# One split quarter in place of two, and a new order for all steps, in a fused RWKV attention and feed-forward kernel

## The chip, the core and the metric

The kernel runs on one core of a Trainium2 chip. The core has a matrix engine (TensorE, PE in the profile), three engines for elementwise work (VectorE or DVE, ScalarE or ACT, GpSimd or POOL) and an engine that mostly sends transfers (SyncE, SP). Each engine takes its own instructions strictly in the order in which the program lists them; engines wait for one another through semaphores. Transfers between device memory and the on-chip memory SBUF run on 16 DMA engines, which all queues share. The metric is the device time of one execution in microseconds.

## The reference

There are two parts. The first is a linear attention with a decaying state, over 4 batches, 8 heads, 768 time steps and a head width of 48. The second is a feed-forward layer (3072 tokens, 384 to 2048 to 384) with a smooth gate.

```python
for t in range(S):
    kt, vt, rt = (k[:, :, t].copy(), v[:, :, t].copy(), r[:, :, t].copy())
    cur = np.einsum('bhd,bhe->bhde', u[None] * kt, vt)
    y[:, :, t] = np.einsum('bhd,bhde->bhe', rt, state + cur)
    state = w[None, :, :, None] * state + np.einsum('bhd,bhe->bhde', kt, vt)
...
h = x @ w_in
g = np.where(pos, h, np.where(neg, 0.0, (h + beta) ** 2 / (4.0 * beta)))   # pos: h >= 1, neg: h <= -1
return (g @ w_out).astype(np.float32)
```

## The kernel before

Time is cut into 6 chunks of 128 steps, and the 4 batches into 2 pairs, which gives 12 groups, numbered 0 to 11. A group has two units (one batch each), so units run from 0 to 23. A unit is 128 tokens, a group 256. Within a chunk the recurrence becomes matrix products, and from chunk to chunk only a state per batch is carried.

For a group the steps are, by the names that the code and this text use:
- `load.K`, `load.R`, `loadV` (line 304): SP brings in K, R and V. Groups 0 and 1 come in two halves (192 KB), the others whole (384 KB).
- `Ks`, `Rs` (327): K and R times powers of the decay. `KU`, `RKU` (337, 344): the products whose row sums, `usum` (357), are the diagonal term. `V` (a cast, 212) and `V2` (367 or 369), V times the diagonal.
- `T` and `TT` (388, 212), in groups 0 to 2: TensorE turns Ks and Rs, and an engine copies them out. From group 3 on, SP does it with transposing transfers, `KRT.K` and `KRT.R` (398).
- `A` (406), `AT` (412, 416 or 421): the product of turned K and R, and its causal mask. `AT.n.0` is one VectorE instruction; where `AT.n.1` stands, ScalarE copies and POOL masks afterwards.
- `Sp`, `Tm`, `decay`, `sbf` (432, 476 and 484, 489, 212): the update of the state. `Y` and `y` (441 and 446, 468): the attention output. `X`, `xT` (501, 212 or 511): it is turned.
- `mm1.g.q` (526): the first layer of group g, quarter q of its 2048 columns, 12 matmuls for both units (written with a last figure of -1), or two halves, one for each unit, where the quarter is split. `relu`, `square`, `gate` (534 and 539 on ScalarE, 544 on VectorE) make the gated quarter, and `mm2.g.j.q` (554, 4 matmuls) adds its part of the second layer for unit j. `o` and `out` copy the sum and store it.

The weights are sent by POOL: `w_in` in two halves (290; half 0 holds quarters 0 and 1, half 1 quarters 2 and 3) and `w_out` in four (294).

The order of all this is a table of steps, written out as text in `ORDER`. The kernel walks through it and emits each step's instructions; each engine then has its instructions in that order. A step reads `name.arguments@engine:buffers~fillers`: the engine is D, P or A, the digits choose buffers, and the last figure is a number of matmuls on zeros put ahead of the step, to keep TensorE running. `warm.n` is n such matmuls by themselves.

```python
for token in ORDER.split():
    token, _, idles = token.partition("~")
    idle[0] = int(idles or 0)
    name, _, bufs = token.partition(":")
    name, _, e = name.partition("@")
    kind, *args = name.split(".")
    if kind == "warm":
        keep_warm(int(args[0]), *args[1:])
    elif kind in do:
        do[kind](e, [int(x, 36) for x in bufs], *[int(x) if x.lstrip("-").isdigit() else x for x in args])
```

The table itself was made outside the kernel by a planner, whose rules are not part of the file.

Of the kernel before, what the change touches and what calls it, by code (L numbers as in the profile page):

```python
# [40 lines left out]
usum.1.0@A:1 A.1:0~8 V2.0.0@P:0 Ks.2.0@P:2 AT.2.0:1 loadV.2.0:0 V2.1.0@A:1 Y.0:1 T.3:2 sbf.0@A Tm.2@D usum.0.1@D Y.2:0
TT.3@D:3 y.2:0 AT.1.1:2 Rs.2.0@P:2 A.3:1~14 X.2:0 V2.0.1@A y.0:1 AT.3.0:3 warm.2.h.2 X.0:1 T.5:2~8 AT.1.0 xT.2@A:0
T.4:0 TT.5@D:0 Y.1:0 w_in.1 load.K.3.0:0 xT.0@A:1 sbf.1@A usum.1.1@D A.5:1 mm1.0.0.0:2 KU.2.0@P:0 y.1:2 TT.4@D:1
load.R.3.0:0 V.1.1@A X.1:1 Y.3:0 AT.5.0:0 A.4:0 V2.1.1@P xT.1@A mm1.0.0.1 V.2.0@A:2 Sp.5:1 y.3:0 RKU.2.0@P:0
relu.0.0:0 X.3:0 Tm.5@D:0 mm1.0.1.0:1 AT.4.0:1 xT.3@A decay.5 square.0.0:0 usum.2.0@D:0 Sp.4:1 mm1.0.1.1 w_out.0 Y.4:0
relu.0.1:1 mm1.1.1.-1:0 gate.0.0:0 square.0.1:1 Tm.4@D:1 mm1.0.2.-1:2 relu.1.1:0 Y.5:1 square.1.1:0 V2.2.0@P:0 w_out.1
y.4:1 gate.0.1:1 w_out.2 X.4:0 w_out.3 mm1.0.3.-1:1 xT.4@A:2 gate.1.1:2 relu.0.2:1 Sp.3:0 y.5:2 mm1.1.0.-1:0
square.0.2:1 Tm.3@D KU.3.0@P:1 decay.4 gate.0.2:3 relu.0.3:0 relu.1.0:1 mm2.0.0.0:1 mm2.0.1.0:0 Ks.3.0@P:0 RKU.3.0@D:1
square.1.0:0 KRT.K.3:0 mm1.1.3.-1:2 mm2.0.1.1 Rs.3.0@P:0 mm2.0.0.1 square.0.3:1 gate.1.0:4 mm2.0.1.2 gate.0.3:5
relu.1.3:1 loadV.3.0:1 mm2.0.0.2 mm1.1.2.-1:0 square.1.3:0 usum.3.0@D:1 mm2.0.0.3 relu.1.2:0 KRT.R.3:0 mm2.0.1.3  # L50
o.0.0@D:0 square.1.2:1 mm2.1.0.0:1 o.0.1@D gate.1.3:6 load.K.4.0:1 X.5:0 mm2.1.0.1 load.R.4.0:1 xT.5@A V.3.0@A:3
mm1.2.3.-1:1 gate.1.2:7 sbf.3@A V2.3.0@P:1 Sp.7:0 A.7:2 loadV.4.0:0 relu.2.3:1 Tm.7@D:0 A.6:0 mm2.1.0.2 AT.6.0:2
sbf.2@A square.2.3:0 Ks.4.0@P:2 sbf.4@A Sp.6:0 mm2.1.0.3 load.K.5.0:2 Tm.6@D:1 mm1.2.0.-1:0 o.1.0@A:1 AT.7.0:3 decay.6
Y.6:0 Y.7:1 relu.2.0:0 KRT.K.4:1 y.6:0 mm1.2.1.-1:2 KU.4.0@P:0 y.7 V.4.0@A:4 gate.2.3:8 xT.6:1 RKU.4.0@P:0
square.2.0:1 mm2.1.1.0:0 Sp.8:1 mm2.1.1.1 load.R.5.0:2 Tm.8@D:1 relu.2.1:1 load.K.6.0:0 mm1.2.2.-1:1 gate.2.0:9
Ks.5.0@P:1 mm2.1.1.2 square.2.1:0 mm2.2.0.0:1 mm2.1.1.3 decay.7 Rs.4.0@P:1 mm1.3.0.-1:0 gate.2.1:0 relu.2.2:0
square.2.2:1 KRT.K.5:0 mm2.2.0.1 o.1.1@D sbf.5@A relu.3.0:1 mm1.3.1.-1:2 gate.2.2:1 out.1 KU.5.0@P:1 square.3.0:0
Rs.5.0@P:2 mm2.2.0.2 relu.3.1:0 gate.3.0:3 mm1.3.2.-1:1 KRT.R.4:1 square.3.1:1 loadV.5.0:1 load.R.6.0:0 usum.4.0@D:0
mm2.2.0.3 mm2.2.1.0:0 KU.6.0@P:0 relu.3.2:1 gate.3.1:5 mm1.3.3.-1:0 square.3.2:0 loadV.6.0:0 gate.3.2:4 mm2.2.1.1
V2.4.0@P:0 sbf.6@A o.2.0@A:1 A.9:2 sbf.7@A relu.3.3:0 A.8:1 AT.9.0:1 mm2.2.1.2 KRT.R.5:0 square.3.3:1 mm2.3.0.0:1  # L60
AT.8.0:0 out.0 decay.8 mm2.2.1.3 load.K.7.0:1 mm2.3.0.1 o.2.1@A gate.3.3:2 V.6.0@A:0 V.5.0@A:2 Y.8:0 Ks.6.0@P:0
mm2.3.0.2 y.8:1 Y.9:0 mm2.3.0.3 y.9 RKU.5.0@P:1 A.11:2 xT.8:0 o.3.0@A:0 A.10:1 usum.5.0@D:1 AT.11.0:2 mm2.3.1.0:0
Sp.10:1 KRT.K.6:1 mm2.3.1.1 Rs.6.0@P:0 RKU.6.0@P:0 Tm.10@D:0 mm2.3.1.2 load.R.7.0:1 Sp.9:1 mm2.3.1.3 Tm.9@D:1
V2.5.0@P:1 mm1.4.0.-1:0 AT.10.0:3 o.3.1@A sbf.8@A decay.9 decay.10 KRT.R.6:1 usum.6.0@D:0 relu.4.0:1 Sp.11:1 Y.10:0
mm1.4.1.-1:2 square.4.0:0 Tm.11@D:1 y.10:0 V2.6.0@P:0 Ks.7.0@P:2 Y.11:1 mm1.4.2.-1:1 loadV.7.0:0 out.2 relu.4.1:0
gate.4.0:7 y.11 A.12:0 xT.10:2 square.4.1:1 AT.12.0:0 mm2.4.0.0:0 Sp.12:1 relu.4.2:1 KU.7.0@P:1 square.4.2:0
gate.4.1:6 load.K.8.0:2 mm1.4.3.-1:0 V.7.0@A:1 KRT.K.7:0 gate.4.2:9 load.R.8.0:2 A.13:2 Rs.7.0@P:1 mm2.4.0.1 out.3
Tm.12@D:0 mm1.5.0.-1:1 AT.13.0:1 RKU.7.0@P:1 relu.4.3:0 square.4.3:1 relu.5.0:1 gate.4.3:0 loadV.8.0:1 square.5.0:0
sbf.9@A decay.12 mm2.4.0.2 Y.12:1 mm1.5.2.-1:2 usum.7.0@D:1 mm2.4.0.3 Ks.8.0@P:1 y.12:1 mm1.5.1.-1:0 gate.5.0:1
o.4.0@A:1 Y.13:1 KRT.R.7:0 relu.5.2:0 V2.7.0@P:1 KRT.K.8:1 Sp.13:0 square.5.2:1 mm1.5.3.-1:1 y.13 Tm.13@D:0 decay.11  # L70
relu.5.1:1 xT.12:1 gate.5.2:8 mm2.4.1.0:1 KU.8.0@P:0 Sp.14:0 square.5.1:0 mm2.4.1.1 load.K.9.0:0 Tm.14@D:1 mm2.4.1.2
relu.5.3:0 sbf.10@A gate.5.1:3 mm2.5.0.0:0 Rs.8.0@P:2 A.15:2 square.5.3:1 A.14:0 AT.15.0:3 mm2.4.1.3 mm2.5.0.1
V.8.0@A:3 KRT.R.8:1 decay.13 RKU.8.0@P:0 AT.14.0:2 mm1.6.0.-1:2 o.4.1@A load.R.9.0:0 gate.5.3:5 Y.14:1 mm2.5.0.2
Ks.9.0@P:0 y.14:0 relu.6.0:1 mm1.6.1.-1:0 square.6.0:0 usum.8.0@D:0 gate.6.0:4 loadV.9.0:0 load.K.10.0:1 mm2.5.0.3
mm2.5.1.0:1 sbf.11@A sbf.12@A A.17:1 relu.6.1:0 o.5.0@D:0 KU.9.0@P:1 A.16:2 mm2.5.1.1 AT.17.0:0 V2.8.0@P:0 decay.14
Rs.9.0@P:0 square.6.1:1 sbf.13@A Y.15:0 mm2.5.1.2 mm1.6.2.-1:1 y.15 V.9.0@A:4 AT.16.0:1 xT.14:0 KRT.K.9:0 Sp.15:0
RKU.9.0@P:1 gate.6.1:2 mm2.5.1.3 load.R.10.0:1 mm1.6.3.-1:2 relu.6.2:1 square.6.2:0 relu.6.3:0 o.5.1@D Tm.15@D:0
mm2.6.0.0:1 gate.6.2:7 out.5 Y.16:0 mm1.7.1.-1:0 decay.15 square.6.3:1 y.16:1 KRT.R.9:0 Ks.10.0@P:2 Sp.17:0 Tm.17@D:1
gate.6.3:6 load.K.11.0:2 mm2.6.0.1 relu.7.1:1 mm1.7.0.-1:1 KU.10.0@P:0 square.7.1:0 sbf.15@A mm2.6.0.2 Sp.16:0
relu.7.0:0 KRT.K.10:1 loadV.10.0:1 gate.7.1:9 mm1.7.2.-1:2 Rs.10.0@P:1 Tm.16@D:0 mm2.6.0.3 square.7.0:1 o.6.0@A:0  # L80
# [557 lines left out]
```

## Time and profile before

| what | value |
|---|---|
| median of 3 runs | 174.3 us (174.28 to 174.5) |
| the profiled execution | 174.08 us |
| its span, first to last instruction | 172.4 us |
| granted TensorE clock | 1.000 |
| TensorE busy | 163.6 us, 95% |
| VectorE, ScalarE, POOL busy | 78%, 79%, 69% |
| bytes moved by DMA | 28.78 MB |

All times in the rows are microseconds from the span's start, unless a row says ns. A row of a timeline gives start, length, engine, line, operation and what is written from what; in brackets stands how long the engine sat idle before, and what ended that. A row of a group gives the count, the time busy, the mean of one in ns, and the idle time before. The busy share of TensorE counts the matmuls on zeros as well.

### The profile page before, as it was taken

The page shows a single profiled execution, that of the slowest core. Times are in us where ns is not written, and L with a number is a line of the kernel's source. Part 1 is how long each engine was busy: PE and PEld are TensorE (multiplying, and loading weights), DVE is VectorE, ACT ScalarE, POOL GpSimd, SP SyncE. Part 2 cuts the span into 40 slices and gives each one's busy share as a digit, 9 for nine tenths or more (in the row PEclk, how much of TensorE's full clock was granted, in tenths as well). Part 3 has the DMA queues.
Part 4 walks back from the last instruction along what each step waited for, and adds up shares of the span by engine and source line. Part 5 has one row for each costly group of instructions (what it writes and reads, how often), then busy time and mean ns, then how long its engine had stood idle before and what let it go on. Part 6 is the DMA issues. An engine that isn't in the chain of part 4 may idle for free.

```text
span 172.4 us, 4127 instructions
## 1 busy us (share of the span) xinstructions
PE 163.6 (95%) x1668; PEld 123.6 (72%) x1668; DVE 133.6 (78%) x167; ACT 135.4 (79%) x194; POOL 118.2 (69%) x96
## 2 busy tenths in 40 slices
...
DMA packets 106967, 28.78 MB, mean 167 GB/s; under 512 B 100930, under 2 KB 106180, under 8 KB 106948
## 3 DMA queue, kind: packets, MB, share of 16 engines
...
q10 hardware_dynamic: 148, 0.10, 0.2%
q14 instruction: 6, 0.05, 0.1%
...
## 4 chain that ended last, share of the span: by engine, by line
PE 73%; DMA 7%; DVE 6%; POOL 5%; SPq 4%; ACT 2%; issue 1%; DVEq 0%; POOLq 0%
PE op L554 32%; PE hp L526 32%; DMA w_in_sb<-in_moe_w_in_dram 5%; SPq L304 4%; PE A L406 3%; DVE RKU L344 2%; DMA R<-in_r_dram 2%; DVE AT L421 2%; PE Y L446 2%; PE Y L441 2%; DVE gt L544 2%; PE Sp L432 1%; POOL AT L416 1%; POOL Rs L327 1%; POOL Ks L327 1%
## 5 line engine op out<-in xcount | busy, mean ns | idle before, releaser
L526 PE MATMUL hp<-xT,w_in_sb 128*128 128x256 bf16 (+1 forms) x600 | 70.8, 268 | 1.2 <-DMA w_in_sb<-in_moe_w_in_dram 0.4
L554 PE MATMUL op<-w_out_sb,gt 128*128 128x384 bf16 x384 | 71.8, 326 | 0.1
L544 DVE SCALAR_TENSOR_TENSOR gt<-sq,hp 128x1024 bf16<-128x1024 f32 x48 | 57.9, 1216 | 14.5 <-ACT sq L539 14.4
L526 PEld LDWEIGHTS <-w_in_sb 128*128 128x128 bf16 x600 | 55.6, 98 | 11.3 <-issue 1.2
L534 ACT ACTIVATE pt<-hp 128x1024 f32<-128x1024 f32 x48 | 48.7, 1019 | 12.0 <-PE hp L526 11.8
L539 ACT ACTIVATE sq<-pt 128x1024 f32<-128x1024 f32 x48 | 50.4, 1057 | 2.8 <-DVE gt L544 1.6
L554 PEld LDWEIGHTS <-gt 128*128 128x128 bf16 x384 | 35.6, 98 | 20.0 <-issue 0.6
L421 DVE TENSOR_TENSOR AT<-A,umask 128x1024 bf16<-128x1024 f32 x22 | 26.5, 1218 | 1.9 <-PE A L406 1.7
L337 POOL TENSOR_TENSOR KU<-K,u_bc 128x768 f32<-128x768 f32 (+1 forms) x13 | 21.7, 1667 | 1.8 <-DVE u_bc L212 1.8
L369 POOL TENSOR_TENSOR V<-V,diag 128x768 f32<-128x768 bf16 (+1 forms) x12 | 16.5, 1375 | 8.8 <-ACT V L212 7.1
L344 POOL TENSOR_TENSOR RKU<-R,KU 128x768 f32<-128x768 f32 (+1 forms) x13 | 20.4, 1575 | 0.4 <-DMA R<-in_r_dram 0.2
L489 POOL TENSOR_TENSOR state<-Tm,wCm 128x384 f32<-128x384 f32 x16 | 16.1, 1006 | 5.3 <-DVE Tm L476 5.1
L327 POOL TENSOR_TENSOR Ks<-Wdn,K 128x768 bf16<-128x768 f32 x10 | 18.3, 1831 | 0.9 <-DMA K<-in_k_dram 0.9
L327 POOL TENSOR_TENSOR Rs<-Wup,R 128x768 bf16<-128x768 f32 x10 | 18.3, 1826 | 0.0
L468 DVE TENSOR_TENSOR yy<-Y,V 128x384 bf16<-128x384 f32 x18 | 9.9, 553 | 5.0 <-PE Y L446 3.5
L212 ACT COPY oo<-op 128x384 f32<-128x384 f32 x13 | 6.2, 477 | 7.9 <-PE op L554 7.9
L446 PE MATMUL Y<-V,AT 128*128 128x48 bf16 x192 | 11.2, 184 | 1.2 <-POOL AT L416 0.9
L212 ACT CAST V<-VF 128x768 bf16<-128x768 f32 (+1 forms) x14 | 10.2, 736 | 2.6 <-DMA VF<-in_v_dram 2.6
L446 PEld LDWEIGHTS <-AT 128*128 128x128 bf16 x192 | 9.5, 96 | 2.7 <-POOL AT L416 1.2
L476 DVE TENSOR_TENSOR Tm<-Sp,state 128x384 f32<-128x384 f32 x16 | 8.9, 554 | 3.1 <-PE Sp L432 1.8
L357 DVE TENSOR_REDUCE diag<-RKU 128x16 f32<-128x768 f32 (+1 forms) x13 | 11.1, 851 | 0.0
L212 ACT CAST state_bf<-state 128x384 bf16<-128x384 f32 x20 | 10.0, 503 | 0.0
...
## 6 DMA issues: line engine op xcount, KB each, us to landing
out_dram<-oo SPq DMA_DIRECT2D x11, 384.0 KB, 3.1
K<-in_k_dram SPq DMA_DIRECT2D x10, 384.0 KB, 4.6
R<-in_r_dram SPq DMA_DIRECT2D x10, 384.0 KB, 4.5
VF<-in_v_dram SPq DMA_DIRECT2D x10, 384.0 KB, 5.3
...
w_out_sb<-in_moe_w_out_dram POOLq DMA_DIRECT2D x4, 384.0 KB, 7.4
K<-in_k_dram SPq DMA_DIRECT2D x4, 192.0 KB, 3.6
R<-in_r_dram SPq DMA_DIRECT2D x4, 192.0 KB, 3.9
```

Source lines behind the costliest of these rows:

```text
L212: nc.scalar.copy(out, in_) if e == "A" else engines[e].tensor_copy(out, in_)
L327: engines[e].tensor_mul(of_unit(dst, j0, j1)[:, :, :, :D], rep(tab, j1 - j0), of_unit(tiles[what, g], j0, j1))
L337: engines[e].tensor_mul(of_unit(tiles["KU", g], j0, j1), of_unit(tiles["K", g], j0, j1), rep(u_bc, j1 - j0))
L344: engines[e].tensor_mul(of_unit(tiles["RKU", g], j0, j1), of_unit(tiles["R", g], j0, j1), of_unit(tiles["KU", g], j0, j1))
L369: engines[e].tensor_mul(tiles["V2", g][:, hs, :], tiles["V", g][:, hs, :], tiles["diag", g][:, hs].unsqueeze(2).to_broadcast([P, hs.stop - ...
L421: nc.vector.tensor_mul(t.rearrange("p i n t -> p (i n) t"), tiles.pop(("A", n)).rearrange("p i n t -> p (i n) t"), umask.unsqueeze(1).to_b ...
L446: nc.tensor.matmul(t[:, 2 * p + i, :], tiles["AT", n][:, i, p, :], tiles["V", g][:, j * H + 2 * p + i, :], start=(c == 0), stop=True, skip ...
L526: nc.tensor.matmul(hp[:, f, cols], w_in_sb[:, i, n0 : n0 + P], tiles["xT", g][:, units, i, :], start=(i == 0), stop=(i == nK - 1), skip_gr ...
L534: nc.scalar.activation(tiles["pt", g, q], tiles["hp", g, q], AF.Relu, bias=0.5, scale=0.5)
L539: nc.scalar.activation(tiles["sq", g, q], tiles.pop(("pt", g, q)), AF.Square, bias=0.0)
L544: nc.vector.scalar_tensor_tensor(out=gt, in0=tiles.pop(("sq", g, q)), scalar=1.0, in1=tiles.pop(("hp", g, q)), op0=ALU.min, op1=ALU.max)
L554: nc.tensor.matmul(tiles["op", g, j], tiles["gt", g, q][:, f, j * P : (j + 1) * P], w_out_sb[:, n, :], start=(n == 0), stop=(n == nF - 1),)
```

## The change

`SPLIT` goes from 2 to 1; no line of the kernel reads it, and it records what the table was made with. The table is new from its second line on. In group 0 only quarter 0 of the first layer is still in halves, and quarter 1 is one piece. Some steps change engine: KU.0.0, RKU.0.0 and RKU.1.1 go from POOL to VectorE, RKU.3.0 from VectorE to POOL, TT of units 2, 3 and 4 from VectorE to ScalarE, usum.1.0 from ScalarE to VectorE, V2.0.1 from ScalarE to POOL, and ten of the copies of outputs between ScalarE and VectorE. The number of matmuls on zeros goes from 62 to 75. The other steps are the same ones in another order.

```diff
-SPLIT = 2
+SPLIT = 1
...
-lw loadV.0.0:0 bcw:1 load.K.1.1 KU.0.1@D loadV.0.1 wcol:0 Wdn_p:0 Ks.0.0@D:0 Wup_p load.R.1.1 Rs.0.0@D:0 wCm
+loadV.0.0:0 KU.0.0@D:0 loadV.0.1 RKU.0.0@D:0 bcw:1 wcol:0 Wdn_p:0 KU.0.1@D load.R.1.1 Wup_p Ks.0.0@D:0 KU.1.0@P:1
...
```

On POOL, from its last product of the first group's second half, up to the second half of w_in (V with a number is a V2; AFFINE_SELECT is the mask of AT; L290 sends w_in):

```order
 L344 TENSOR_TENSOR RKU<-R,KU 128x384
+L369 TENSOR_TENSOR V_254<-V,diag 128x384
+L416 AFFINE_SELECT AT<-AT 128x1024
 L290 DMA w_in_sb<-in_moe_w_in_dram 128x3x1024
-L416 AFFINE_SELECT AT<-AT 128x1024
-L369 TENSOR_TENSOR V_327<-V,diag 128x384
 L327 TENSOR_TENSOR Ks<-Wdn,K 128x16x48
 L327 TENSOR_TENSOR Rs<-Wup,R 128x16x48
 L416 AFFINE_SELECT AT<-AT 128x1024
+L369 TENSOR_TENSOR V_254<-V,diag 128x384
+L369 TENSOR_TENSOR V_343<-V,diag 128x384
 L290 DMA w_in_sb<-in_moe_w_in_dram 128x3x1024
```

The first send of w_in now comes after the V2 and the mask of unit 0, and the second after the V2 of the other half of group 0 and of the second half of group 1.

On VectorE, in groups 0 and 1 (tab holds the powers of the decay; diag is usum; state from Sp is Tm of the first chunk):

```order
 L357 TENSOR_REDUCE diag<-RKU 128x8
-L327 TENSOR_TENSOR Ks<-tab,K 128x8x48 x2
+L327 TENSOR_TENSOR Ks<-tab,K 128x8x48
+L327 TENSOR_TENSOR Rs<-tab,R 128x8x48
+L484 TENSOR_TENSOR state<-Sp,wCm 128x384
+L344 TENSOR_TENSOR RKU<-R,KU 128x384
+L357 TENSOR_REDUCE diag<-RKU 128x8
+L484 TENSOR_TENSOR state<-Sp,wCm 128x384
 L212 COPY TT<-T 128x1024
```

RKU.1.1 now stands here, behind the first state and ahead of the copy TT of unit 1. Further on, in the gates of group 0 and 1:

```order
+L468 TENSOR_TENSOR y<-Y,V_638 128x384
 L544 SCALAR_TENSOR_TENSOR gt<-sq,hp 128x1024
-L344 TENSOR_TENSOR RKU<-R,KU 128x768
+L468 TENSOR_TENSOR y<-Y,V_638 128x384
 L544 SCALAR_TENSOR_TENSOR gt<-sq,hp 128x1024 x2
```

The whole-group product RKU.3.0 is gone from between the gates.

On SP, where group 3 is turned (KT and RT) and groups 3 and 4 are loaded:

```order
 L304 DMA R<-in_r_dram 128x16x48
 L398 DMA_TRANSPOSE KT<-Ks 128x8x128
+L304 DMA K<-in_k_dram 128x16x48
 L304 DMA VF<-in_v_dram 128x16x48
 L398 DMA_TRANSPOSE RT<-Rs 128x8x128
+L304 DMA R<-in_r_dram 128x16x48
```

The load of K for group 4 now goes between the transposes of group 3, ahead of V for group 3.

More of the change, by code (lines that the diff above doesn't have):

```diff
@@ L41 @@
[L41 to L80, printed above, removed]
@@ L96 @@
-mm2.10.0.0:1 relu.11.0:0 mm2.10.1.1 square.11.0:0 square.11.1:1 mm2.10.0.1 gate.11.0:4 relu.11.2:0 mm2.10.1.2
-square.11.2:0 mm2.10.0.2 mm2.10.1.3 out.9 mm2.10.0.3 mm1.11.3.-1:1 o.10.0@D:0 o.10.1@D gate.11.1:2 out.10 mm2.11.0.0:1
-relu.11.3:1 mm2.11.1.0:0 gate.11.2:7 square.11.3:1 mm2.11.0.1 mm2.11.1.1 gate.11.3:6 mm2.11.0.2 mm2.11.1.2 mm2.11.0.3
-o.11.0@D:0 out.11.0 mm2.11.1.3 o.11.1@A:1 out.11.1
+warm.18 load.K.0.0:0 load.R.0.0:0 load.K.0.1 load.R.0.1 load.K.1.0:1 load.R.1.0:1 load.K.1.1 bcu:0 lw u_bc@D
```

81 lines of the change are left out of this document (62 added, 19 removed).

## The prediction

> **What bounds the kernel now.** I read the page first, for the span and the share of each engine, then the chain of waits in order of time, and then each engine's timeline where the chain leaves TensorE. From the page:
>
> ```profile
> span 172.4 us, 4127 instructions
> PE 163.6 (95%) x1668; PEld 123.6 (72%) x1668; DVE 133.6 (78%) x167; ACT 135.4 (79%) x194; POOL 118.2 (69%) x96
> ```
>
> TensorE (PE) is the bound by share, but the filler matmuls count in it, so I go by stretches. From the chain of waits (start, length, what):
>
> ```profile
> 8.30 3.82 DMA R<-in_r_dram
> ...
> 20.55 8.09 DMA w_in_sb<-in_moe_w_in_dram
> ...
> 28.69 1.48 PE hp L526 x12
> ...
> 34.41 3.97 DVE RKU L344
> ...
> 39.56 1.47 PE hp L526 x12
> ...
> 45.35 0.17 PE Sp L432 x4
> 45.52 0.55 PE A L406 x16
> ...
> 47.65 1.31 PE hp L526 x12
> ...
> 49.70 1.31 PE hp L526 x12
> 51.01 0.65 PE op L554 x4
> ...
> 163.50 5.21 PE op L554 x32
> 168.74 0.48 ACT o_sb L567
> ```
>
> These rows cut the span into three stretches and give each step's price on TensorE: a first-layer quarter (mm1, 12 matmuls) 1.31 us, a second-layer step (mm2, 4 matmuls) 0.65, Sp 0.17, A 0.275 (two in 0.55), and one Y 0.37 (two stand between 48.96 and 49.70).
> - Up to 28.69 TensorE waits for its first work. The last wait there is for the second half of w_in, sent at 20.55; it lets mm1.0.2 start at 28.69.
> - From 28.69 to 47.65 (mm1.2.0) lie 6 quarters, 12 mm2 steps, one Y, three Sp, two A and two X (taken as 0.17, like Sp): 7.86 + 7.80 + 0.37 + 0.51 + 0.55 + 0.34 = 17.4 of 18.96 us. So 1.5 us are stalls, and the chain shows where: RKU of group 3, 3.97 us on VectorE, holds the gate that releases the matmul at 39.56.
> - From 47.65 to the last matmul's end at 168.71 lie 39 quarters, 84 mm2 steps, 18 Y, 12 Sp and 16 A: 51.1 + 54.6 + 6.7 + 2.0 + 4.4 = 118.8 of 121.1 us, so 2.3 us are stalls. Then 3.7 us of tail.
>
> The change leaves this work as it is from mm1.2.0 on. What can differ is when mm1.2.0 starts, the later stalls, and the tail.
>
> **The change, part by part.** *The split quarter.* mm1.0.1 was two halves and becomes one piece. The timeline of PE for halves:
>
> ```profile
> 21.39 0.84 PE L526 MATMUL hp<-xT,w_in_sb 128*128 128x128 bf16 x12
> 22.07 0.33 PE L501 MATMUL X<-ident,y 128*128 128x128 bf16 x3
> ```
>
> A half takes 0.68 us from start to start, two take 1.36 against 1.31: 0.05 us. It lies ahead of a wait (below), so I count nothing. The 13 further fillers (75 for 62, at 0.06 to 0.11 us each) stand ahead of waits too: nothing.
>
> *When the weights are sent.* This is the main term. POOL sends w_in, in its order, and before it ran so:
>
> ```profile
> 13.20 0.93 POOL L290 DMA_DIRECT2D w_in_sb<-in_moe_w_in_dram  x1
> ...
> 15.19 0.84 POOL L369 TENSOR_TENSOR V<-V,diag 128x384 f32<-128x384 bf16 x1
> ...
> 17.75 1.82 POOL L327 TENSOR_TENSOR Rs<-Wup,R 128x768 bf16<-128x768 f32 x1
> 19.52 1.09 POOL L416 TENSOR_SCALAR_AFFINE_SELECT AT<-AT 128x1024 bf16<-128x1024 bf16 x1
> 20.55 0.80 POOL L290 DMA_DIRECT2D w_in_sb<-in_moe_w_in_dram  x1
> ...
> 28.92 2.29 POOL L294 DMA_DIRECT2D w_out_sb<-in_moe_w_out_dram  x3
> ```
>
> Now w_in.0 stands behind V2.0.0 and the mask of AT.0, and w_in.1 behind V2.0.1 and V2.1.1. POOL loses three half-size products to VectorE (KU.0.0, RKU.0.0, RKU.1.1) and gains V2.0.1 (0.84 us, as the row at 15.19), which ScalarE did. ScalarE's rows:
>
> ```profile
> 11.71 1.01 ACT L412 CAST AT<-A 128x1024 bf16<-128x1024 f32 x1
> ...
> 22.18 0.51 ACT L212 CAST V<-VF 128x384 bf16<-128x384 f32 x1 [0.82 <-DMA VF<-in_v_dram]
> ```
>
> AT.0.1 at 11.71 follows the cast of the second half of V0, whose load keeps its place in the queue, so I leave it at 11.8. Its end at 12.8, the mask's 1.1 (row at 19.52), and w_in.0 goes at 13.9 to 14.1, 0.7 to 0.9 late. Then Ks.2 (15.0) and Rs.2, each 1.82 as the row at 17.75 (to 18.6), the mask of AT.1 (19.6), V2.0.1 (20.4). V2.1.1 needs the cast V.1.1, at 22.18 before and waiting for its load. That load meets the weights. Issues on SP and issues to landing:
>
> ```profile
> 9.30 0.94 SPq L304 DMA_DIRECT2D VF<-in_v_dram  x1
> ...
> 11.06 1.73 SPq L304 DMA_DIRECT2D R<-in_r_dram  x1
> 12.83 3.55 SPq L304 DMA_DIRECT2D VF<-in_v_dram  x2
> ```
> ```profile
> VF<-in_v_dram SPq DMA_DIRECT2D x1, 192.0 KB, 3.6
> ```
> ```profile
> R<-in_r_dram SPq DMA_DIRECT2D x1, 384.0 KB, 6.3
> ```
> ```profile
> VF<-in_v_dram SPq DMA_DIRECT2D x1, 192.0 KB, 9.3
> ```
>
> V1.0 lands at 12.9 and R2 at 17.4, two loads of 384 KB later (K2 lies between): 2.2 us each. V1.1, half of that, would land at 18.5; it landed at 22.1, when w_in.0 had gone through (13.20 and the 8.1 us of w_in in the chain is 21.3). So loads of SP hardly move while weights do. With w_in.0 0.7 to 0.9 later V1.1 just misses or just makes it. I take that most of it is caught again and it lands at 21.5 to 22. Then V.1.1 ends at 22.1, V2.1.1 at 22.9, and w_in.1 goes 2.3 us late, at 22.9; with the 8.1 us of the first chain row it lands at 31.0. TensorE is ready by then: w_in.0 lands at 22.1, three quarters follow (3.9), and the steps for Y and X between them, with their casts, bring it to the end of Y.4 at about 29; this has 2 us of room and does not carry the sum. So mm1.0.2 starts at 31.0, 2.3 us late. Bounds: w_in.1 at 21.4 (V1.1 in time, POOL alone the limit), 0.9 late; and 23.5, 3 late.
>
> *From there to mm1.2.0.* Y.5 is now done ahead of mm1.0.2, and one Sp (0.17) too: 16.9 us remain. RKU.3.0 goes back to POOL, where a product of that size takes 1.83 us (row at 33.95, below), so the 3.97 us on VectorE are gone. From the page, ScalarE's two steps for a quarter (count, busy, mean ns):
>
> ```profile
> L534 ACT ACTIVATE pt<-hp 128x1024 f32<-128x1024 f32 x48 | 48.7, 1019 | 12.0 <-PE hp L526 11.8
> L539 ACT ACTIVATE sq<-pt 128x1024 f32<-128x1024 f32 x48 | 50.4, 1057 | 2.8 <-DVE gt L544 1.6
> ```
>
> That is 2.08 us a quarter. Five quarters go through ScalarE between 31.0 and the gate of mm1.1.3, which TensorE wants last, at about 47: 10.4 us of 16, with room for the small casts and the gate; I find no stall there. What is late next is group 3 on SP, where load K4 now stands between the two transposes, ahead of V3:
>
> ```profile
> 35.81 1.33 SPq L398 DMA_TRANSPOSE KT<-Ks  x1
> 37.25 0.52 SPq L304 DMA_DIRECT2D VF<-in_v_dram  x1
> 37.86 3.47 SPq L398 DMA_TRANSPOSE RT<-Rs  x1
> ```
> ```profile
> KT<-Ks SPq DMA_TRANSPOSE x1, 5.1
> ```
> ```profile
> VF<-in_v_dram SPq DMA_DIRECT2D x1, 384.0 KB, 5.4
> ```
> ```profile
> RT<-Rs SPq DMA_TRANSPOSE x1, 5.6
> ```
>
> They land in turn: KT at 40.9, V3 at 42.6, RT at 43.5; so a load of 384 KB takes about 1.8 us of the stream, a transpose 0.9. w_out's last piece was sent by 31.2 (row at 28.92); now KU.2, RKU.2, a decay, V2.2 and four sends follow w_in.1, so it is sent by about 33. The stream, busy with w_in.1 until 31.0, sets its end rather than the sending; I take 1 us later, so KT lands at 41.9, K4 at 43.7, V3 at 45.5, RT at 46.4. TensorE, without stalls, would ask for V3 (Sp.6) at 45.7; cast (0.83 us) and RT give it at 46.5. That is 0.8 us lost. mm1.2.0 starts at 31.0 + 16.9 + 0.8 = 48.7, 1.1 us late. From both sides: if the loads run as fast as they did before it is nothing, if K4 waits for w_out's end longer, 2 us.
>
> *From mm1.2.0 on.* POOL has two products of 1.8 us less left (Ks.4 and KU.4 are done earlier), so what feeds the attention steps is further ahead. I take 0.6 of the 2.3 us of stalls as gone; the ends are all of them (2.3) and 2 us more. Copies of the output that change engine are ten and balance. At the end the two units swap names and stand in the same order: nothing.
>
> **Sum:** 1.1 - 0.6 = 0.5 us. The profiled execution took 174.08 us around its span of 172.4; the median shown, 174.3, is 0.2 above it. So 174.6 for such an execution, and 174.8 as a median. The forecast's own range is 174.2 to 175.6.
>
> **The rivals.** *V1.1 slips ahead of the weights* (faster). It needs about 1.1 us more of the stream than R2, and gets 0.7 to 0.9, with R2's 17.4 already somewhat held up. If it lands by 20, w_in.1 goes at 21.5, mm1.0.2 starts at 29.6, w_out keeps its old times, and V3 and RT land at 44.6 and 45.7; mm1.2.0 then starts at 47.8, 0.15 late, and with 0.6 of stalls gone the time is 173.8. The later stalls vanishing whole would bring either case a further 1.7 us.
>
> *RKU.1.1 caught behind POOL* (slower). The product has two operands in SBUF, as the 3.97 us one had, and POOL ran two products beside that one:
>
> ```profile
> 33.95 1.83 POOL L327 TENSOR_TENSOR Ks<-Wdn,K 128x768 bf16<-128x768 f32 x1
> 35.73 1.83 POOL L327 TENSOR_TENSOR Rs<-Wup,R 128x768 bf16<-128x768 f32 x1
> ```
>
> It began at 34.41 and ended at 38.38, 0.8 us after POOL's second had ended at 37.56: it stood still until POOL paused. RKU.1.1 comes up at 12.2 (its load lands at 12.1, the first row of the chain). POOL pauses at 12.5, before AT.0's mask; a start there costs nothing. From 12.85 on POOL's queue is closed up to the end of Rs.2 at 18.6; a VectorE that is 0.4 us later than I reckon stands until then, with TT.1 and AT.2 behind it: 5.6 us, of which the 2.3 us of waiting for w_in.1 hide some: 178. [...]
>
> *ScalarE becomes the bound in groups 2 and 3* (slower). Between mm1.2.0 and mm1.3.3 TensorE has 6 quarters, 12 mm2 steps, 3 Y, 2 Sp and 2 A: 17.7 us. ScalarE has six relu and six square there, 12.5 us, and eight smaller steps, where the old order had six and five, and three smaller ones. If it comes into this stretch over 2 us behind, each gate waits for its square: about 2 us, 176.5. Against it speaks ScalarE's share, 79% on the page, and that two of the eight steps are casts whose loads come early.
>
> *It comes to nothing:* the times move within the ramp and the same end is reached, 174.0 to 174.6.
>
> **How the numbers follow.** Forecast 0.40, V1.1 in time 0.24, ScalarE 0.18, nothing 0.10, RKU.1.1 caught 0.08. The three stalls of unknown size give the range: 173.0 (V1.1 in time and half of the later stalls gone besides) to 177.3 (ScalarE with 0.8 more), which leaves out the caught RKU and a little below. No change is within 0.2% (0.35 us), about what a measurement of this kernel can tell. Faster: 0.24 and 0.06 of the forecast with all later stalls gone, 0.30. Same: 0.10 and 0.08 of the forecast's lower edge, 0.18. Slower: 0.26 + 0.18 + 0.08 = 0.52.
>
> **What would show it.** Right: POOL's second w_in issue near 22.9, V.1.1's cast waiting for its load, TensorE waiting for w_in shortly before 31, no VectorE product of several us, and a wait for V3 or RT near 46. Wrong: the second issue by 21.6 with V1.1 landed by 20; RKU.1.1 on VectorE longer than 1.5 us; ScalarE named as what the gates wait for between 49 and 66; or stalls after mm1.2.0 that sum to over 3 us.

## The result, and the profile after

The changed kernel took 177.01 us (three runs, 176.16 to 177.57) where the kernel before took 174.3. The ratio is 1.0137, with a 95% interval from 1.0104 to 1.017: slower, by 2.7 us where 0.5 was forecast. The profiled execution after took 177.01 us around a span of 175.3, so the span grew by 2.9 us. In every median and ratio here and below, executions that took over 1.5% longer than the fastest of the same kernel are left out; three of them, in two of the runs below, took 212 to 417 us.

From the page, the span, TensorE's share, and the granted clock by fortieths of the span (4.4 us each):

```profile
span 175.3 us, 4111 instructions
PE 165.0 (94%) x1669; PEld 125.5 (72%) x1669; DVE 131.2 (75%) x168; ACT 134.9 (77%) x172; POOL 117.8 (67%) x95
PEclk9999969999999999999999999999999999999998
```

The sixth digit is new (the row before was all nines): from 21.9 to 26.3 us TensorE got 0.69 of its clock. The same stretch by 2 us (length, busy time of PE, PEld, DVE, ACT, POOL with counts, clock, DMA):

```profile
22.00:24.00 2.00, 0.72 (x14) 0.64 (x14) 1.94 (x3) 1.68 (x4) 1.12 (x2) 0.90 1.12 222
24.00:26.00 2.00, 2.00 (x13) 1.36 (x10) 1.75 (x3) 0.83 (x1) 1.98 (x2) 0.50 1.22 228
26.00:28.00 2.00, 2.00 (x28) 1.85 (x26) 0.24 (x1) 1.28 (x2) 1.92 (x2) 0.75 1.18 201
```

POOL, where it sends the two halves of w_in (its timeline):

```profile
13.77 0.93 POOL L290 DMA_DIRECT2D w_in_sb<-in_moe_w_in_dram  x1
...
22.88 0.83 POOL L369 TENSOR_TENSOR V<-V,diag 128x384 f32<-128x384 bf16 x1 [2.19 <-ACT V L212]
23.65 0.80 POOL L290 DMA_DIRECT2D w_in_sb<-in_moe_w_in_dram  x1
```

The second half goes at 23.65; it went at 20.55. Ahead of it POOL stood 2.19 us for V2.1.1, that is for the cast of V1.1, which stood on ScalarE for its load. The load itself was not later than before, when the cast began at 22.18; new is what stands behind it.

```profile
22.29 0.51 ACT L212 CAST V<-VF 128x384 bf16<-128x384 f32 x1 [1.95 <-DMA VF<-in_v_dram]
22.71 0.85 ACT L212 COPY xT<-X 128x384 bf16<-128x384 bf16 x2
```

The transfer of the second half takes 8.1 us from issue to landing, so the weights are there at 31.75:

```profile
w_in_sb<-in_moe_w_in_dram POOLq DMA_DIRECT2D x1, 768.0 KB, 8.1
```

TensorE's timeline, from that wait to mm1.0.2 and then at mm1.2.0:

```profile
23.23 0.33 PE L432 MATMUL Sp<-V,Ks 128*128 128x96 bf16 x4 [1.23 <-ACT xT L212]
23.61 0.48 PE L446 MATMUL Y<-V,AT 128*128 128x48 bf16 x8
23.91 3.63 PE L526 MATMUL hp<-xT,w_in_sb 128*128 128x256 bf16 x24
...
29.63 0.20 PE L441 MATMUL Y<-state_bf,TT 128*128 128x96 bf16 x1 [0.62 <-ACT xT L212]
...
31.68 0.77 PE L204 MATMUL hp<-zeros 128*128 128x128 bf16 x11
32.30 1.91 PE L526 MATMUL hp<-xT,w_in_sb 128*128 128x256 bf16 x16
...
47.72 0.33 PE L432 MATMUL Sp<-V,Ks 128*128 128x96 bf16 x4 [0.40 <-ACT V L212]
...
50.02 1.47 PE L526 MATMUL hp<-xT,w_in_sb 128*128 128x256 bf16 x12
```

The row at 32.30 is mm1.0.2: it waits for nothing, so in this execution TensorE itself came last, 0.55 us after the weights. The chain of waits agrees (start, length, what): it leads from the load of V1.1 through ScalarE and TensorE to the matmuls on zeros ahead of mm1.0.2, and not through w_in.

```profile
13.02 9.25 DMA VF<-in_v_dram
22.29 0.51 ACT V L212
22.80 0.77 ACT xT L212 x2
...
26.69 1.03 ACT pt L534
27.74 1.06 ACT sq L539
...
29.20 0.39 ACT xT L212
...
31.84 0.62 PE hp L204 x11
```

mm1.2.0 is the last row, at 50.02. (The timeline shows it at 47.48 before; the chain of waits, by which the prediction counted, adds 0.16 or 0.17.) The increase splits like this:

| stretch | before | forecast change | after | change |
|---|---|---|---|---|
| to mm1.0.2 | 28.69 | +2.3 | 32.30 | +3.6 |
| mm1.0.2 to mm1.2.0 | 18.8 | -1.2 | 17.7 | -1.1 |
| mm1.2.0 to the span's end | 124.9 | -0.6 | 125.3 | +0.4 |

In the last stretch the only waits of TensorE that the timeline shows are for the turned R of groups 5 and 7:

```profile
72.86 0.62 PE L406 MATMUL A<-RT,KT 48*128 48x128 bf16 x16 [0.62 <-DMA RT<-Rs]
92.88 0.40 PE L406 MATMUL A<-RT,KT 48*128 48x128 bf16 x8 [0.27 <-DMA RT<-Rs]
```

### The profile page after: what moved, and what is told of

It is laid out like the page before. It is cut to its first block, busy times and chain, and to the rows that moved or that the text cites. A ratio compares the mean times of both kernels' runs of the same rounds, so it can differ in the third digit from the quotient of the medians.

```text
span 175.3 us, 4111 instructions
## 1 busy us (share of the span) xinstructions
PE 165.0 (94%) x1669; PEld 125.5 (72%) x1669; DVE 131.2 (75%) x168; ACT 134.9 (77%) x172; POOL 117.8 (67%) x95
## 4 chain that ended last, share of the span: by engine, by line
PE 53%; POOL 14%; DMA 14%; SPq 7%; ACT 6%; issue 3%; DVE 0%; POOLq 0%
PE hp L526 24%; PE op L554 23%; DMA VF<-in_v_dram 9%; SPq L304 7%; POOL Rs L327 3%; POOL Ks L327 3%; DMA RT<-Rs 3%; POOL KU L337 3%; DMA K<-in_k_dram 2%; POOL V L369 2%; POOL state L489 2%; PE A L406 2%; ACT sq L539 2%; PE Y L446 2%; PE Y L441 1%
## 5 line engine op out<-in xcount | busy, mean ns | idle before, releaser
L526 PE MATMUL hp<-xT,w_in_sb 128*128 128x256 bf16 (+1 forms) x588 | 71.9, 274 | 0.0
L554 PE MATMUL op<-w_out_sb,gt 128*128 128x384 bf16 x384 | 71.0, 326 | 0.0
L526 PEld LDWEIGHTS <-w_in_sb 128*128 128x128 bf16 x588 | 56.2, 99 | 10.1 <-DMA xT<-yy 0.3
L534 ACT ACTIVATE pt<-hp 128x1024 f32<-128x1024 f32 x48 | 49.0, 1020 | 17.5 <-PE hp L526 17.3
L421 DVE TENSOR_TENSOR AT<-A,umask 128x1024 bf16<-128x1024 f32 x22 | 26.3, 1217 | 1.9 <-PE A L406 1.8
L369 POOL TENSOR_TENSOR V<-V,diag 128x768 f32<-128x768 bf16 (+1 forms) x13 | 17.3, 1328 | 11.3 <-ACT V L212 8.2
L337 POOL TENSOR_TENSOR KU<-K,u_bc 128x768 f32<-128x768 f32 (+1 forms) x12 | 20.2, 1686 | 4.6 <-DMA K<-in_k_dram 4.6
L212 ACT COPY oo<-op 128x384 f32<-128x384 f32 x12 | 5.6, 476 | 6.3 <-PE op L554 6.3
```

The costliest lines, as they stand in the source:

```text
L212: nc.scalar.copy(out, in_) if e == "A" else engines[e].tensor_copy(out, in_)
L337: engines[e].tensor_mul(of_unit(tiles["KU", g], j0, j1), of_unit(tiles["K", g], j0, j1), rep(u_bc, j1 - j0))
L369: engines[e].tensor_mul(tiles["V2", g][:, hs, :], tiles["V", g][:, hs, :], tiles["diag", g][:, hs].unsqueeze(2).to_broadcast([P, hs.stop - ...
L421: nc.vector.tensor_mul(t.rearrange("p i n t -> p (i n) t"), tiles.pop(("A", n)).rearrange("p i n t -> p (i n) t"), umask.unsqueeze(1).to_b ...
L526: nc.tensor.matmul(hp[:, f, cols], w_in_sb[:, i, n0 : n0 + P], tiles["xT", g][:, units, i, :], start=(i == 0), stop=(i == nK - 1), skip_gr ...
L534: nc.scalar.activation(tiles["pt", g, q], tiles["hp", g, q], AF.Relu, bias=0.5, scale=0.5)
```

## The experiments

In the diffs each line is one token of the table of steps, cut to the place; dots stand for tokens left out. The table shows for every run where three marks of TensorE lie in its profile (start of mm1.0.2, start of mm1.2.0, end of the span), and the time against the kernel before on the same chip. The medians of before were 174.7 to 174.9 on those chips. Executions of one changed kernel spread by a microsecond or two. The marks are those of one profiled execution each: they show where its time went, and carry that spread too. The steps behind mm1.2.0 are the same in seven of the runs with the new order (after and six others), and there the rest alone goes from 125.3 to 127.0.

| run | mm1.0.2 | mm1.2.0 | end | rest | median | ratio and interval |
|---|---|---|---|---|---|---|
| before | 28.69 | 47.48 | 172.4 | 124.9 | 174.3 | 1 |
| after | 32.30 | 50.02 | 175.3 | 125.3 | 177.01 | 1.0137 (1.0104 to 1.017) |
| before, w_in.1 late | 32.32 | 51.72 | 176.7 | 125.0 | 177.53 | 1.0165 (1.0111 to 1.0218) |
| before, RKU.3.0 on POOL | 28.98 | 47.34 | 172.4 | 125.1 | 174.42 | 0.9979 (0.9959 to 1.0) |
| before, quarter in one piece | 29.14 | 47.81 | 173.0 | 125.2 | 174.87 | 1.0011 (0.9991 to 1.003) |
| after, w_in.1 sooner | 31.17 | 48.80 | 175.6 | 126.8 | 177.27 | 1.011 (1.0037 to 1.0183) |
| after, V1.1 hidden | 33.06 | 50.81 | 176.7 | 125.9 | 178.09 | 1.0184 (1.0143 to 1.0225) |
| after, both | 31.15 | 48.99 | 174.3 | 125.3 | 177.78 | 1.0202 (1.0163 to 1.0241) |
| after, 26 fillers | 32.23 | 49.78 | 176.8 | 127.0 | 179.34 | 1.025 (1.0202 to 1.0299) |
| after, K4 later | 32.31 | 49.87 | 176.8 | 126.9 | 178.3 | 1.0189 (1.0142 to 1.0236) |
| after, send between the V2, fewer fillers | 30.82 | 48.89 | 175.0 | 126.1 | 176.86 | 1.0107 (1.0027 to 1.0187) |
| that, and V1.1 hidden | 29.48 | 48.36 | 174.8 | 126.4 | 176.64 | 1.0101 (1.0068 to 1.0135) |
| that, and two late moves | 30.35 | 49.01 | 174.8 | 125.8 | 176.52 | 1.0113 (1.007 to 1.0157) |
| after, two late moves alone | 31.55 | 49.84 | 175.3 | 125.5 | 177.31 | 1.0195 (1.0118 to 1.0272) |

### The late send by itself

The theory to be tested first was that the late second send of w_in is the cost; the rival, that V1.1's held load is, through ScalarE and the clock. The kernel before got the late send and nothing else:

```diff
 Y.1:0
-w_in.1
 load.K.3.0:0
...
 V2.1.1@P
...
+w_in.1
```

> The kernel before with only the second send of w_in put behind KU.2 and V2.1.1 on POOL, at 23.9 us in place of 20.55. Theory A: the weights land at 32, mm1.0.2 starts 3.3 us late, of which the stall behind RKU.3.0 (its end at 38.4 does not move) takes back 1: 176.5. Theory B: the send by itself is a third of the loss at most: 175.0 to 175.5.

The send went at 23.97. TensorE's timeline:

```profile
27.48 1.47 PE L526 MATMUL hp<-xT,w_in_sb 128*128 128x256 bf16 x12
32.32 2.08 PE L526 MATMUL hp<-xT,w_in_sb 128*128 128x256 bf16 x12 [3.37 <-DMA w_in_sb<-in_moe_w_in_dram]
```

mm1.0.2 comes 3.6 us late, after a plain wait of 3.37 us for the weights, and the end is 4.3 us later (the first quarters behind the wait ran at a low clock, 0.76 from 32 to 34 us and 0.50 from 34 to 36, the first in 2.08 us against 1.47). The ratio, 1.0165, is that of the changed kernel within the uncertainty: one late send is enough for the whole increase, which speaks for theory A (176.5) and against theory B (175.5 at most).

### Curing one limit of the changed kernel, or both

First w_in.1 alone, ahead of both V2 products (sent at 20.39):

```diff
+w_in.1
 V2.0.1@P
...
 V2.1.1@P
...
 Sp.3:1
-w_in.1
```

> The changed kernel with one step moved: POOL sends the second half of w_in ahead of V2.0.1 and V2.1.1, at about 19.9 us in place of 23.65. Theory A (the late send is what costs): the weights land by 28.5, mm1.0.2 starts 2 us sooner, time 175.0. Theory B (the load of V1.1, held by the first half of w_in, stops ScalarE for 2 us and with it the start of the first layer, and TensorE's clock drops while it waits): TensorE itself reaches mm1.0.2 only at about 32, so nothing moves, 176.5 to 177.2.

Then V1.1 alone: the first quarter goes ahead of Sp.3, and ScalarE copies xT of units 2 and 1 before it casts V1.1 (w_in.1 then goes at 24.88):

```diff
-V.1.1@A
 A.5:0
 xT.2@A:1
-V2.1.1@P
...
 xT.1@A
+mm1.0.1.-1:1
+V.1.1@A
+V2.1.1@P
 Sp.3:1
...
-mm1.0.1.-1:1
```

> The changed kernel with the wait for V1.1 put behind the first quarter: ScalarE casts V.1.1 after xT of units 2 and 1, and TensorE runs mm1.0.1 before Sp.3 and Y.3. Nothing else moves. Theory A (late send): the second half of w_in still lands at 31.7, so 176.5 to 177. Theory B: mm1.0.1 starts at about 22.3 in place of 23.9 with the clock up, and TensorE then waits for w_in at mm1.0.2 until 31.8: 0.5 us gained, 176.5. By both the gain alone is small; a wait for w_in at mm1.0.2 must appear by B and not by A.

And both moves:

> Both of the two moves together. Theory A: as the sooner send alone, 175.0. Theory B: only together do they help, mm1.0.2 at about 29 in place of 32.3, 3 us gained, of which V3 and the transposed R of group 3 take back 1: 175.0. The two theories part on the sooner send alone, not here; if this too stays at 177, neither holds and the loss lies in group 3 and behind it.

With the weights sooner there was no wait for w_in, and yet mm1.0.2 started at 31.17 only, as theory B said and not theory A. This move is no clean cure, though: V2.0.1 now stood behind the send, and TensorE waited 1.10 us at 22.71 for y of unit 1, in place of the wait for V1.1. With V1.1 hidden TensorE was ready at 31.52 and stood 1.54 us for the weights, the wait that theory B asked for:

```profile
33.06 1.16 PE L526 MATMUL hp<-xT,w_in_sb 128*128 128x256 bf16 x9 [1.54 <-DMA w_in_sb<-in_moe_w_in_dram]
```

The 33.06 itself is not the price of the move: in that execution R of group 2 landed late (Rs.2 began at 18.27, in the changed kernel's profile at 17.03), and what follows on POOL and TensorE was as much later. So two limits lie within about a microsecond of each other, the weights and TensorE itself, and curing one uncovers the other. With both moves mm1.0.2 still starts at 31.15, where 29 was expected, since the wait for y of unit 1 is there as in the run with the send alone. The time stayed near 177.8 where both theories gave 175.0, so this run decides nothing between them:

```profile
22.47 0.34 PE L501 MATMUL X<-ident,y 128*128 128x128 bf16 x3 [1.11 <-DVE y L468]
...
23.69 1.47 PE L526 MATMUL hp<-xT,w_in_sb 128*128 128x256 bf16 x12 [0.55 <-DVE AT L421]
```

### The clock

In the changed kernel's profile 24 matmuls (the first quarter and half of the second) took 3.63 us, at half clock up to 27 us (0.50). The two other executions of the changed kernel kept a mean clock of 1.000 and took 176.16 and 177.57 us, so the increase does not hang on the clock. If the wait of 1.23 us ahead of the matmuls lowers it, matmuls on zeros should prevent it:

```diff
-Sp.3:1
+Sp.3:1~26
```

> The changed kernel with 26 more matmuls on zeros ahead of the state product Sp.3, where TensorE stood idle for 1.23 us before its clock fell to half. Theory: the wait for V1.1 costs through the clock; the fillers (26 at about 0.055 us, 1.4 us) lie in the idle time and keep the clock up. Then the 24 matmuls of the first quarter take about 2.15 us instead of 3.63, TensorE reaches mm1.0.2 at about 30.8 instead of 32.30, and only now waits for the second half of w_in, about 0.9 us, to 31.75: mm1.0.2 at 31.8, mm1.2.0 at 49.5, time 0.5 us less than the changed kernel's. First rival: the idle time is not what lowers the clock; the 24 matmuls take 3.6 us again, mm1.0.2 stays at 32.3 or goes to 32.5. Second rival: the weights come earlier too and the whole 1.5 us is gained, mm1.0.2 at 30.8.

```profile
23.29 1.61 PE L204 MATMUL Sp<-zeros 128*128 128x128 bf16 x26 [1.01 <-ACT xT L212]
24.73 0.33 PE L432 MATMUL Sp<-V,Ks 128*128 128x96 bf16 x4
...
25.11 2.14 PE L526 MATMUL hp<-xT,w_in_sb 128*128 128x256 bf16 x24
```

The 24 matmuls took 2.14 us, but the experiment missed its aim: the row shows that the fillers wait for the copy xT too (they write the buffer of Sp.3, which has the same figure as that of X of unit 2), and behind it they cost 1.44 us of their own. The next runs settle the question in another way. The one below has the changed order up to 39.5 us, with the same wait, longer still, and the clock stayed up:

```profile
24.05 0.33 PE L432 MATMUL Sp<-V,Ks 128*128 128x96 bf16 x4 [1.57 <-ACT xT L212]
24.64 2.14 PE L526 MATMUL hp<-xT,w_in_sb 128*128 128x256 bf16 x24
...
32.31 1.92 PE L526 MATMUL hp<-xT,w_in_sb 128*128 128x256 bf16 x16 [0.39 <-DMA w_in_sb<-in_moe_w_in_dram]
```

There mm1.0.2 waits for w_in and starts at 32.31, as late as before (the send was at 24.47). In the run with the two late moves alone, further down, it also waits for w_in, and starts at 31.55. So the low clock is no steady part of the change; with it or without it the late weights let mm1.0.2 start at 31.55 to 32.31.

### K of group 4 back behind V of group 3

```diff
-load.K.4.0:0
 square.0.3:1
...
 loadV.3.0:1
...
 KRT.R.3:0
...
+load.K.4.0:0
 Ks.4.0@P:1
```

> The changed kernel with one load moved on SP: K of group 4 goes behind V and the second transpose of group 3, not between them. Theory (a term of the prediction): K4 ahead of V3 holds V3 and RT of group 3 back by 0.8 us and TensorE waits for them ahead of mm1.2.0. Then V3 lands at about 46.0 instead of 46.8, RT at 47.0 instead of 47.8, and from mm1.0.2 to mm1.2.0 go 17.0 us instead of 17.7; time 0.8 us less than the changed kernel's. Rival: K4 then lands so late that POOL's Ks.4 (which waited 2.27 us for it already) and with it the later products on POOL slip by 2 to 3 us; the 0.8 us come back as waits for A and T after mm1.2.0, and the time stays at 177.

The wait for V3 (0.40 us in the changed kernel) is gone, but mm1.0.2 to mm1.2.0 shortens only from 17.7 to 17.6 us. Behind it the rival's waits came: 0.97 us at 54.37 behind y on VectorE and 0.86 at 74.21 for the turned R, and the rest grew to 126.9. POOL now has K of group 4 at 48.6 and starts Ks.4 3.8 us later than in the changed kernel (48.7 for 44.88).

### Two single steps done to the kernel before

RKU of group 3 on POOL, behind Rs of group 3:

```diff
 Ks.3.0@P:0
-RKU.3.0@D:1
...
 Rs.3.0@P:0
 mm2.0.0.1
+RKU.3.0@P:1
```

> The kernel before with one step of the change: the product RKU of group 3 on POOL, behind Rs of group 3, instead of on VectorE between two gates. Theory: its 3.97 us on VectorE hold a gate back and cost TensorE most of the 1.5 us of stalls between mm1.0.2 and mm1.2.0. On POOL it takes 1.84 us in idle time. Then mm1.0.2 stays at 28.7, mm1.2.0 goes from 47.5 to 46.4 (46.0 to 46.8), and the time from 174.3 to 173.2. Rival: the stall is followed by the wait for V3 and the turned R of group 3, which do not come sooner; mm1.2.0 stays within 0.3 of 47.5 and the time at 174.3.

The quarter in one piece:

```diff
-mm1.0.1.0:1
+mm1.0.1.-1:1
...
-mm1.0.1.1
```

> The kernel before with the one edit that the change's name tells of: quarter 1 of group 0's first layer in one piece instead of two halves, at the place of the first half. Theory: two halves cost 0.05 us more than one piece, both parts of xT are there by then, and it lies ahead of the wait for the weights: 174.3, mm1.0.2 at 28.7. Rival: the piece waits for xT of the second unit, or holds its PSUM buffer longer, and the first relu comes later: ScalarE and the gates of group 0 slip by up to 0.7 us, 175.0.

RKU.3.0 on POOL takes mm1.0.2 to mm1.2.0 from 18.8 to 18.4 us, not the 1.1 us less that was expected. There was little more to gain: in the kernel before, TensorE stood idle only 0.35 us behind that product:

```profile
39.56 1.47 PE L526 MATMUL hp<-xT,w_in_sb 128*128 128x256 bf16 x12 [0.35 <-DVE gt L544]
```

In the execution with RKU.3.0 on POOL the weights were 0.3 us later. The time is 0.2% less, with the interval's upper end at no change; it is the only version of this study with a median below that of the kernel before, by 0.4 us, and that is not clear of the uncertainty. The quarter in one piece is within the uncertainty: 1.0011, interval 0.9991 to 1.003.

### All three early costs at once

Of the 11 us between 21.3 and mm1.0.2 about 4 are waits, fillers and the low clock in the changed kernel, the rest is work. So the second send went between the two V2 products, where it holds up neither, and the 16 matmuls on zeros behind the first quarter went out:

```diff
 V2.0.1@P
...
+w_in.1
 V2.1.1@P
...
-w_in.1
...
-warm.5.h.2
...
-mm1.0.2.-1:1~11
+mm1.0.2.-1:1
```

> The changed kernel with the second half of w_in sent between the two V2 products (so behind V2.0.1 and ahead of V2.1.1), and without the 16 matmuls on zeros that stand between the first quarter and mm1.0.2. The steps stay in the changed order otherwise, so the wait for V1.1 stays. Theory: of the 10.97 us from 21.33 to 32.30 on TensorE, 6.7 are work, 1.23 the wait for xT behind V1.1, 0.62 the wait for xT.3, 0.9 the fillers and 1.5 the low clock. With the fillers gone and the send at 20.7 (landing 28.8) mm1.0.2 starts at 29.9 at full clock and 31.4 at the low one, without a wait for w_in; mm1.2.0 at 47.5 to 49.0; the time 1 to 2.4 us under the changed kernel's. Rival: the weights and the small loads share the transfer engines so that something else lands as much later (R of group 2, V of group 2, the turned products); mm1.0.2 stays above 31.5.

and then the first quarter ahead of Sp.3 as well, as in the run with V1.1 hidden:

> As the run before it, and besides the first quarter of the first layer put ahead of the state product Sp.3, with the cast of V1.1 on ScalarE behind the copies xT of units 2 and 1, so that neither waits for V1.1. Theory: all three costs are gone, the wait for V1.1, the late send, the fillers. The first quarter waits only for its PSUM buffer, until about 22.6 to 22.9; TensorE is at mm1.0.2 at 28.5 to 29.0, about when the weights land (28.8); mm1.0.2 at 28.8 to 29.3, mm1.2.0 at 46.4 to 46.9, which is 0.6 to 1.1 us sooner than in the kernel before, and the time 173.5 to 175. Rival: as in the two runs that cured one or two of the three, something else comes in its place (y of unit 1, the mask of unit 3, V of group 2), mm1.0.2 at 30.5 to 31.2 and the time at 176 to 177.

mm1.0.2 started at 30.82 and 29.48, without a wait for w_in. The second is 2.8 us sooner than in the changed kernel's profile, most of the 3.6; the run with two late moves, further down, has the same early order and 30.35, which is 2.0 sooner. So for the first stretch it is shown that the late send, the wait for V1.1 and the matmuls on zeros together make most of the delay. The matmuls on zeros were not taken out alone, and the low clock of the changed kernel's profile (1.5 us) did not recur, so their shares are not separated. But the end moved by 0.5 us only (175.3 to 174.8), although mm1.2.0 had moved by 1.7, and the ratio (1.0101, to 1.0135) is not clear of the changed kernel's (1.0137, from 1.0104). TensorE behind mm1.2.0 in the last run:

```profile
57.70 2.78 PE L526 MATMUL hp<-xT,w_in_sb 128*128 128x256 bf16 x24 [1.08 <-DMA xT<-yy]
72.43 0.62 PE L406 MATMUL A<-RT,KT 48*128 48x128 bf16 x16 [0.61 <-DMA RT<-Rs]
```

It stands for the turned R of group 5 until 72.43; without any cure it stood there until 72.86. In the changed kernel this wait ended 22.8 us behind mm1.2.0, and 22.9 to 23.1 in the three runs that cured one limit or both: there it still followed mm1.2.0, and with both moves the end did too (174.3, rest 125.3). In the last two runs, with mm1.2.0 at 48.9 and 48.4, it ended 23.6 and 24.1 us behind, so there something else holds it.

### Two late moves

POOL makes Ks of group 6 ahead of Ks and Rs of group 5, and SP issues the transpose of K of group 4 ahead of xT.6. Both were turned round, first in the changed kernel alone, then together with the early cures:

```diff
-KRT.K.4:1
...
 xT.6:0
+KRT.K.4:1
...
-Ks.6.0@P:2
...
 Rs.5.0@P:2
+Ks.6.0@P:2
```

> The changed kernel with two moves behind mm1.2.0 and none ahead of it: on POOL, Ks of group 6 goes behind Rs of group 5 instead of ahead of Ks of group 5; on SP, the transpose of group 3's output (xT.6) goes ahead of the transpose of K of group 4. Theory: in the changed order POOL makes Ks.6 before Ks.5 and Rs.5, so the turned R of group 5 lands at 72.4 to 72.9 whatever happened before, and TensorE waits there (0.62 us in the changed kernel); and xT.6 stands behind a transfer that SP takes up to 4 us to issue. With both moved the wait for RT at 72.9 is gone; mm1.2.0 stays at 50.0, the end is 0.6 us sooner, 176.4. Rival: the wait at 72.9 only covers others that come right behind it (RT of group 6, the turned K of group 4); the time from mm1.2.0 to the end stays at 125.3 or goes to 126.

> The run with all three early cures (send between the V2 products, no fillers, first quarter ahead of the wait for V1.1) and besides the two late moves of the run before. Theory: the early cures brought mm1.2.0 to 48.4 but the end only to 174.8, since TensorE then waited 1.08 us for xT.6 and 0.61 for the turned R of group 5 at 72.43, the same place in time as without the cures. With both waits gone the end follows mm1.2.0: 48.4 plus 124.8 is 173.2 of span, 175.0 in time (1.9 less than without the late moves). Rival: TensorE is not what is late there, other waits of POOL's and DMA's chain come in their place, and the span stays at 174.5 to 175.

The wait for xT.6 did not return, but the one for the turned R did: 0.71 us until 72.78, and 0.91 until 72.14. Rs of group 5 was done 2 us sooner, at 65.3 and 64.7, and that did not help, because SP came to it only at 68.1 and 67.5. SP's queue in the last run (start, time to issue):

```profile
61.61 2.91 SPq L398 DMA_TRANSPOSE KT<-Ks  x1
64.62 0.53 SPq L304 DMA_DIRECT2D VF<-in_v_dram  x1
65.19 2.16 SPq L304 DMA_DIRECT2D K<-in_k_dram  x1
67.46 2.62 SPq L398 DMA_TRANSPOSE RT<-Rs  x1
```

The load of K for group 7 stands ahead of the transpose and takes 2.16 us to issue. The theory that POOL's order holds that R fell; in these two traces SP's order holds it, which no run tested by moving an entry of SP's. POOL for its part waits for loads too. KU of group 5, first in the changed kernel and then in the run with the three early cures:

```profile
54.27 1.82 POOL L337 TENSOR_TENSOR KU<-K,u_bc 128x768 f32<-128x768 f32 x1 [0.65 <-DMA K<-in_k_dram]
```

```profile
53.88 1.82 POOL L337 TENSOR_TENSOR KU<-K,u_bc 128x768 f32<-128x768 f32 x1 [1.55 <-DMA K<-in_k_dram]
```

From there POOL works to 74 with one break of 0.7 us, in both within half a microsecond of the same times (in the run with both moves TensorE's wait for the turned R of group 5 ended a microsecond sooner, at 71.91). In the kernel before POOL has no wait for K there. So behind mm1.2.0 the changed order has a second chain, SP's queue and POOL, that runs close to TensorE: the changed kernel's chain of waits leaves TensorE and goes from the load of K for group 6 (56.13) through POOL and the turned R of group 7 back to TensorE at 92.88. TensorE's rest was 125.3 to 127.0 us in every kernel with that order, against 124.9 to 125.2 with the old one. That this chain costs the rest is read from the traces; which entry of SP's queue would have to move for all of it to go was not found.

## Why the prediction was right and wrong

The direction and the range held; 2.7 us came where 0.5 was forecast. That the range held is luck: 177.01 lies outside the forecast's own 174.2 to 175.6, and inside the upper end (177.3) only because that end was set for ScalarE as the bound, which did not come. By its steps:

- *The split quarter, nothing.* Right: 1.0011 with its interval around 1. *Fillers, nothing, since they lie ahead of waits.* Wrong for the 11 ahead of mm1.0.2: in the profiled execution no wait was left there, and of their 0.62 us (31.68 to 32.30) 0.55 lay behind the landing of the weights.
- *w_in.1 sent at 22.9 (21.4 to 23.5), landing at 31.0.* Right in mechanism: V1.1's load was long (issued at 13.02, cast at 22.29), V2.1.1 waited for it, and the send behind it. That the first half of w_in is what held the load is not shown: no run moved that send away, and with it at 13.2 to 13.8 the casts that waited for this load began at 22.1 to 23.1, in no order. Mis-sized by 0.75 us: 23.65, just past the bound, since the cast began at 22.3 where 21.6 was taken.
- *TensorE is ready by about 29, 2 us of room, does not carry the sum.* This is the step that failed first. TensorE was ready at 32.30 in the profiled execution. The sum had left out that the same late cast stands ahead of the copies xT on ScalarE, and so stops TensorE itself (1.23 us); 0.62 more went at 29.63, for a copy xT that stands behind the first relu and square on ScalarE; besides came the low clock (1.5 us) and the fillers. In two runs with the same early order and the clock up, mm1.0.2 waited 0.39 and 0.57 us for w_in, so the room was about half a microsecond. The wait for w_in that the prediction named as its sign was in those two and not in the profiled execution. Together with the send this makes +3.6 of a forecast +2.3.
- *mm1.0.2 to mm1.2.0 1.2 us shorter: RKU.3.0's stall gone, 0.8 us lost to V3.* The total was right to 0.1 us (17.7), by luck, since two errors cancel. The 1.5 us of stalls were the rest of a sum of unit prices; before, TensorE ran no matmul for 0.52 of the 18.8 us (18.27 busy), 0.35 of them behind RKU.3.0, so its work there was about 0.9 us more than the 17.4 reckoned. RKU.3.0 on POOL alone returned 0.4. After, it worked 17.3 us where 16.9 were reckoned, and lost 0.40 to V3 where 0.8 was; moving K4 back returned only 0.15.
- *From mm1.2.0 on 0.6 us less, because POOL is further ahead.* Wrong by 1.0 us, and wrong in mechanism. The 2.3 us of stalls were such a rest too: before, TensorE ran no matmul for only 0.55 of the 121.2 us behind mm1.2.0, and the one wait that the timeline shows there is that of a first-layer quarter behind VectorE's mask, not for a product of POOL's:

```profile
80.22 1.47 PE L526 MATMUL hp<-xT,w_in_sb 128*128 128x256 bf16 x12 [0.39 <-DVE AT L421]
```

  So there was hardly anything to gain. After, it ran none for 0.94 of 121.6 us. POOL, in the changed kernel:

```profile
44.88 1.83 POOL L327 TENSOR_TENSOR Ks<-Wdn,K 128x768 bf16<-128x768 f32 x1 [2.27 <-DMA K<-in_k_dram]
...
60.41 3.59 POOL L327 TENSOR_TENSOR Ks<-Wdn,K 128x768 bf16<-128x768 f32 x2 [0.74 <-DMA K<-in_k_dram]
...
65.41 1.81 POOL L327 TENSOR_TENSOR Rs<-Wup,R 128x768 bf16<-128x768 f32 x1
```

  It stood 2.27 us for K of group 4, 0.65 for that of group 5 (the row at 54.27) and 0.74 for that of group 6, so Rs of group 5 began 15.4 us behind mm1.2.0 (65.41), where before it was 11.4 (58.88). I had counted POOL's products and not the loads that they wait for, nor the transposes queued behind those loads on SP. The runs with early cures show what this is worth: even with mm1.0.2 at 29.48 the time stayed at 176.6.
- *The rivals.* V1.1 did not slip ahead. ScalarE did not become the bound: between mm1.2.0 and 72 TensorE shows no wait for a gate. RKU.1.1 was not caught:

```profile
11.99 0.87 DVE L344 TENSOR_TENSOR RKU<-R,KU 128x384 f32<-128x384 f32 x1
```

It took 0.87 us where two products of that size that ran while POOL was idle took 0.56, and POOL's mask beside it (12.46 to 13.82) took 1.36 us where the one at 18.79 took 1.09: each was about 0.3 us longer. When the product began, POOL's V2 (11.62, 0.83 us) had 0.46 us left. In the kernel before, KU on POOL at 5.65, begun 0.03 us behind a VectorE product of 0.56, took 1.39 us where the next one took 1.00, and RKU.3.0 on VectorE, with two POOL products beside it, took 3.97 us. Why RKU.3.0 took so much longer no run shows.

The sum by terms: 1.3 us were missed up to mm1.0.2, 0.1 in the middle, 1.0 behind it, 2.4 us together.
